# Second-level Strassen for one more product of the last down projection, early weight sums on VectorE, residual loads on GpSimd's queue

## The chip, the core and the metric

The kernel runs on one core of a Trainium2 chip. The core has TensorE for matmuls (the profile names it PE, and PEld for its weight loads), VectorE (DVE), ScalarE (ACT), GpSimd (POOL) and SyncE (SP), which here only issues DMAs. The metric is the device time of one execution in microseconds; less is better.

## The reference

For 2048 tokens of width 1024, with `_layernorm` over the width:

```python
xn = _layernorm(x)
s = linear_attention(xn, wqkv) @ wo          # 32 heads of 32
g = silu((silu(xn @ w_gate) * (xn @ w_up)) @ w_down)   # inner width 3584
return x + s * g
```

The first three of its lines are the reference's `_A_ref` and `_B_ref` in short; all inputs are bf16.

## The kernel before, in words

**Stages.** The first part (to about 245 us of the span) normalizes x, computes the attention branch and writes s to DRAM (`s_dram`). The feed-forward part then goes over the tokens in two passes of 1024. Each pass has a gate/up stage over 28 keys (14 column groups of 256, gate and up alternating; `emit_a`, `emit_c22`, `emit_b`, `emit_evac`) and a down stage. Every matrix product there is done by Strassen's scheme with 7 products of half size in place of 8: sums of the left operand are made by VectorE or GpSimd, sums of the weights are made once and kept in DRAM.

**The first down stage** (`emit_down`, 413.7 to 498.5 us) has an a-half with the four products that are kept or finished early and a b-half with the other three. Each half goes over two pairs of token tiles (hf). In a pair the second tile follows the first by 6 of 14 steps, so a pair has 20 steps (st); a step has one weight row group k of a tile. The b-half begins with pair hf = 1 at 462.2 us and goes on with hf = 0 at 480.3 us. Its banks come from two pools: four banks tagged "s" and two double banks tagged "d" (`dzw`). A tile's double bank is free when its evacuation (`evac_b`, line 1294 for hf = 1, which writes `dd`) has read it. Ahead of the b-half VectorE makes the left sums S1 to S4 of the next pass (`emit_Ssum`, lines 711 to 714).

**The last down stage** (`emit_down_m`, from 668.7 us) computes the seven products M1 to M7 one after the other, for four tiles t of 128 tokens each side. A product at one level is 4 tiles x 14 matmuls of 512 columns (line 1430). Products in `L2` (1, 2 and 4) use Strassen once more (`l2_M`, `l2_p`, line 1466): seven products of 14 matmuls of 256 columns each. `l2_M` is a generator: it stops after its first two products, so that another product can fill in. A second-level product needs four sums of its left operand (`l2_lhs`, lines 1163 to 1166, on GpSimd) and four sums of its weights. The order is M2 and M1 interleaved, M7, M6, M5, M4, M3. M3 is accumulated in M5's banks. Each finished tile goes through Silu on ScalarE and then `fin`.

**The residual** (`fin`, line 1200 to 1202, and `io_load`). For each of 32 tiles of 128 x 512, `fin` multiplies the gate by s (line 1200), adds x (line 1201), both on VectorE, and issues the store of the result; x and s were loaded by `io_load` into a buffer of two halves, and the result is written into the half that held x. Buffers come from a pool of five, "io"; a load goes into a buffer whose store has landed. Five loads are made ahead of the first down stage, and each `fin` issues the next. The last three tiles use the space of the sums S0 to S2 in place of a buffer of the pool. Stores of the first pass are issued by GpSimd (the last three of them are `deferred` into the first three keys of the last pass), stores of the last pass by SP. All loads are issued by SP.

**Early and late weight sums.** For M2 the second-level weight sums are made in the first down stage from weight tiles that are in SBUF anyway (`l2_early`, line 1132, on GpSimd, in steps 1, 3, ... of hf = 1, and stored with a lag of two weight tiles). For M1 and M4 the weights are loaded again in the last gate/up stage (`l2_load`, line 1111), summed by GpSimd (`l2_sums`, line 1144) and stored (line 1145). These loads take slots of the same pool of eight weight slots ("pk") as the weights of the keys.

**What sets the order.** TensorE, VectorE, ScalarE and GpSimd execute in the order of the program (`manual_schedule`), DMAs on GpSimd's queue among them. SP's order is chosen by the framework's planner in the feed-forward part. An instruction that waits holds up all that stand behind it on its engine.

Of the kernel before, what the change touches and what calls it, by code (L numbers as in the profile page):

```python
# [10 lines left out]
ALU = mybir.AluOpType  # L11
# [10 lines left out]
def kernel(  # L22
# [165 lines left out]
    passes = list(range(NPASS - 1, -1, -1))  # L188
    NWA = NFG // 2
    M_ORDER = (1, 2, 7, 6, 5, 4, 3)  # L190
    L2 = (1, 2, 4)
    L2_ORDER = (1, 2, 5, 6, 7, 4, 3)
    NQ = NFG // 2
    CH = CW // 2
# [757 lines left out]
    with ExitStack() as p3:  # L952
# [143 lines left out]
            eng.tensor_tensor(out=a21.bitcast(F16), in0=a12, in1=S2, op=ALU.subtract)  # L1096
            s_ring[(hf, m)] = (S1, S2, S3)

        l2_q = deque((M, j) for M in L2 if M != 2 for j in range(0, NQ, 2))
        l2_live = deque()  # L1100

        def l2_load():
            M, j0 = l2_q.popleft()
            kd, q = M_PACK[M]
            t = w_slot()
            v = t[:].rearrange("p h a b -> p (h a b)").rearrange("p (b j n) -> p b j n", b=8, n=CH)
            js = range(j0, min(j0 + 2, NQ))
            for j in js:
                for k, b0, b1 in ((0, 0, 7), (1, 1, 6)):
                    src = wd_drams[j][0 if kd == "a" else 1][:, k, q].rearrange("p (c n) -> p c n", n=CH)  # L1110
                    nc.sync.dma_start(out=v[:, b0:b1 + 1:b1 - b0, j - j0, :], in_=src)
            l2_live.append((M, js, v))

        def l2_early(M, j, store):

            t = w_tiles[(passes[0], "b", j)][:].rearrange("p h a b -> p (h a b)")
            q = M_PACK[M][1]
            w = t[:, 0:6 * CW].rearrange("p (k q c n) -> p q k c n", k=2, q=3, c=2)[:, q]
            T = t[:, 6 * CW:8 * CW].rearrange("p (b n) -> p b n", b=4)
            if store:  # L1120
                if M not in l2_drams:
                    l2_drams[M] = dram.tile([P, 7, NQ, CH], BF16, name="l2_%d" % M)
                d = l2_drams[M]
                nc.sync.dma_start(out=d[:, 0:2, j], in_=w[:, :, 0])
                nc.sync.dma_start(out=d[:, 6, j], in_=w[:, 1, 1])
                nc.sync.dma_start(out=d[:, 2:6, j], in_=T)
                return
            r = w.bitcast(F16) if M >= 4 else w
            t1, t2, t3, t4 = [T[:, i].bitcast(F16) for i in range(4)]
            for o_, a_, b_ in ((t1, r[:, 0, 1], r[:, 0, 0]), (t2, r[:, 1, 1], t1), (t3, r[:, 1, 1], r[:, 0, 1]),  # L1130
                               (t4, r[:, 1, 0], t2)):
                nc.gpsimd.tensor_tensor(out=o_, in0=a_, in1=b_, op=ALU.subtract)

        def l2_sums():
            M, js, v = l2_live.popleft()
# [8 lines left out]
                nc.gpsimd.tensor_tensor(out=b(o_), in0=b(a_), in1=b(b_), op=ALU.subtract)  # L1144
            nc.gpsimd.dma_start(out=l2_drams[M][:, :, js.start:js.stop, :], in_=v[:, 0:7, 0:n_, :])

        x_spare, r_spare = [], []

        def l2_bufs(M):
            v = [x[:].rearrange("p a b -> p (a b)").bitcast(F16) for x in x_spare]  # L1150
            if M == 1:
                v = [x[:].rearrange("p h a b -> p (h a b)").bitcast(F16) for x in r_spare]
            v = [x[:, 0:2 * NQ * 2 * P].rearrange("p (s j r n) -> p s j r n", s=2, j=NQ, r=2) for x in v]
            return [v[0][:, 0], v[0][:, 1], v[1][:, 0], v[1][:, 1]]

        def l2_quad(A, j):
            v = A[:, :, j].rearrange("p k (r t n) -> p k r t n", r=2, t=2)
            return v[:, 0, :, 0], v[:, 1, :, 0], v[:, 0, :, 1], v[:, 1, :, 1]

        def l2_lhs(M, A, j, eng):  # L1160
            a11, a12, a21, a22 = l2_quad(A, j)
# [22 lines left out]
        def io_load(after=None):  # L1184
            if not fq:
                return
            p, t, cc = key = fq.pop(0)
            r0 = p * TB2 + t * P
            pool, tg = (sp, "S%d" % len(fq)) if len(fq) < 3 else (iop, "io")
            io = pool.tile([P, 2, CW], BF16, name="io", tag=tg)  # L1190
            gate([nc.sync.dma_start(out=io[:, 0, :], in_=x2[r0:r0 + P, cc * CW:(cc + 1) * CW]),
                  nc.sync.dma_start(out=io[:, 1, :], in_=s_dram[r0:r0 + P, cc * CW:(cc + 1) * CW])],
                 after, sync=True)
            io_tiles[key] = io

# [10 lines left out]
        def emit_down(p, h, base, last, more_S, next_S):  # L1206
# [152 lines left out]
            for hf in (1, 0):  # L1359
                t0, t1 = 2 * hf, 2 * hf + 1  # L1360
                fresh = hf == 0
                endz = last and fresh
                for st in range(NFG if endz else NS):
                    if st == 4:
                        while pend:
                            pend.pop(0)()
                    if hf == 1 and not last and st % 2 == 1 and 2 in L2:
                        if st // 2 < NQ:
                            l2_early(2, st // 2, False)
                        if 0 <= st // 2 - 2 < NQ:  # L1370
                            l2_early(2, st // 2 - 2, True)
                    if st < NFG:
                        step_b(t0, st, fresh)
                        if st == NFG - 1:
                            fins = evac_b(t0, fresh)
                    if st >= LEAD and not endz:
                        step_b(t1, st - LEAD, fresh)
                        if fresh and (st - LEAD) % 2 == 1:
                            load_w_to(base + 2 * NWA + (st - LEAD) // 2 + 2)
                if endz:  # L1380
                    for f in fins:
                        f()
                    finish(t1)
                    break
                fins2 = evac_b(t1, fresh)
                for f in fins:
                    f()
                if fresh:
                    deferred.extend(fins2)
                else:  # L1390
                    for f in fins2:
                        f()

        def emit_down_m(p, h, base):
# [8 lines left out]
            def load(M, q=None):  # L1403

                n_ = max(i for i, key in enumerate(seq) if key[2][0] == M and q in (None, key[2][1])) + 1
                load_w_to(base + n_ + (NPK - 2 if M == 1 and q != 3 else NPK))

            def S3(k):
                return s3_[k // NWA][:, k % NWA]
# [59 lines left out]
            def l2_M(M, A, K, done, fill, in_place, dst=None):  # L1469
# [24 lines left out]
                for r in range(2):  # L1494
                    c0, c1 = c[r]
                    if K is None:
                        nc.scalar.copy(out=c1[:, hi], in_=zy[r][:, lo])
                        nc.scalar.copy(out=c0[:, hi], in_=zy[r][:, hi])
                        nc.scalar.copy(out=c0[:, lo], in_=xw[r][:, lo])
                    else:  # L1500
                        tt(c1[:, hi], zy[r][:, lo], K[2 * r + 1][:, hi])
                        tt(K[2 * r][:, hi] if in_place else c0[:, hi], zy[r][:, hi], K[2 * r][:, hi])
# [1 line left out]
                            tt(c0[:, lo], xw[r][:, lo], K[2 * r][:, lo])  # L1504
                    tt(c1[:, hi], xw[r][:, hi], c1[:, hi])
                fill()
                for r in range(2):
                    l2_p(M, 4, r, A, bk)
                load(M, 2)
                for r in range(2):  # L1510
# [2 lines left out]
                        nc.scalar.copy(out=c1[:, lo], in_=zy[r][:, lo])  # L1513
                    else:
                        tt(c1[:, lo], zy[r][:, lo], K[2 * r + 1][:, lo])
                        done(2 * r + 1, c1)
                    l2_p(M, 3, r, A, bk)
                    if in_place:
# [18 lines left out]
            load_w_to(base + NPK - 2)  # L1537
            KA = kept("kA")
            fins = deque()
            M7, M6, M5 = [], [], []  # L1540
            KB = []

            def fill7():
# [17 lines left out]
                flush(1)  # L1561
            load(7)
            sums(S4, A12, S2, ALU.subtract)
            for j in range(NQ):
                l2_lhs(4, quads(h, 1, 1), j, nc.gpsimd)
            M6 = banks()
            for t in range(TPB):
                prod_t(6, t, M6[t], True)
                tt(KB[t], M6[t], KB[t])
                tt(KA[t], M6[t], KA[t])  # L1570
            load(6)
            M5 = banks()
            for t in range(TPB):
                prod_t(5, t, M5[t], True)
                c = k2([P, CW], FP32, "c22")[:]
                tt(c, M5[t], KB[t])
                fins.append((t + TPB, 1, silu(c, "g22")))
                if len(fins) > 1:
                    flush(1)
            tt(KA[-1], M5[-1], KA[-1])  # L1580
            load(5)

            def out3(t):
                prod_t(3, t, M5[t], False)
                c = k2([P, CW], FP32, "c12")[:]
                tt(c, M5[t], KA[t])
                fins.append((t, 1, silu(c, "g12")))

            def done4(t, c):
                fins.append((t + TPB, 0, silu(c, "g21")))  # L1590

            def fill3():
                flush()
                out3(0)
            go(l2_M(4, quads(h, 1, 1), KB, done4, fill3, True))
            hs_ = [slice(0, 3 * CW // 4), slice(3 * CW // 4, CW)]
            out3(1)
            flush(len(fins) - 1)
# [15 lines left out]
        for pi, p in enumerate(passes):  # L1614
# [69 lines left out]

            na0 = 6 if first else 8
            l2_j = 0
            load_w_to(base + na0)
            if first:
                wd_pipe2(-1)
# [3 lines left out]
            for i in range(n):  # L1693
# [38 lines left out]
                if not first:  # L1732
                    if l2_live:
                        l2_sums()
                    if i in (17, 18):
                        r_spare.append(w_slot())
                    if i % 2 == 1 and l2_q:
                        l2_load()
                    if i >= 18 and 4 * l2_j + 4 <= i:
                        l2_lhs(1, quads(h, 0, 0), l2_j, nc.gpsimd)  # L1740
                        l2_lhs(2, quads(h, 1, 0), l2_j, nc.gpsimd)
                        l2_j += 1
                if deferred:
                    deferred.pop(0)()
            base += n
            if last_pass:
                l2_lhs(2, quads(h, 1, 0), NQ - 1, nc.gpsimd)
# [36 lines left out]
```

## Time and profile before

| | us |
|---|---|
| runs: median (lowest to highest of 3) | 758.43 (756.7 to 759.07) |
| the profiled execution | 756.18 |
| its span in the trace | 754.4 |
| first down stage, a-half / b-half hf = 1 / hf = 0 | 413.7 to 462.2 / to 480.3 / to 498.5 |
| last gate/up stage | 498.5 to 668.7 |
| last down stage, end of the last matmul | 668.7, 749.8 |

All times in the text are microseconds from the start of this span. A line of the profile names an engine, a source line of the kernel, an operation and its tiles (output <- inputs), and how many there were. In a waits view the numbers are the total, the number of waits and the longest. In a timeline they are start and duration, in brackets the engine's idle time before and what ended it. In a DMA view the last number is the median time from issue to landing. SPq and POOLq are DMA issues of these engines.

Other rows that matter here. The granted clock of TensorE is 1.00 in each stretch from 412 to 743.8. VectorE is busy 9.62 of the 18.3 us of hf = 1 of the b-half and 9.80 of the 18.2 us of hf = 0. The DMA engines are busy 0.38 of the a-half, 0.93 of hf = 1, 0.73 of hf = 0 and 0.92 of 498.5 to 523.

### The profile page before, as it was taken

The page shows a single profiled execution, that of the slowest core. Times are in us where ns is not written, and L with a number is a line of the kernel's source. Part 1 is how long each engine was busy: PE and PEld are TensorE (multiplying, and loading weights), DVE is VectorE, ACT ScalarE, POOL GpSimd, SP SyncE. Part 2 cuts the span into 40 slices and gives each one's busy share as a digit, 9 for nine tenths or more (in the row PEclk, how much of TensorE's full clock was granted, in tenths as well). Part 3 has the DMA queues.
Part 4 walks back from the last instruction along what each step waited for, and adds up shares of the span by engine and source line. Part 5 has one row for each costly group of instructions (what it writes and reads, how often), then busy time and mean ns, then how long its engine had stood idle before and what let it go on. Part 6 is the DMA issues. An engine that isn't in the chain of part 4 may idle for free.

```text
span 754.4 us, 11075 instructions
## 1 busy us (share of the span) xinstructions
PE 745.8 (99%) x3857; PEld 360.8 (48%) x3857; DVE 581.4 (77%) x1040; ACT 381.1 (51%) x545; POOL 399.8 (53%) x500
## 2 busy tenths in 40 slices
PE   8999999999999999999999999999999999999997
PEld 3544444454454444444444444444444444467464
DVE  6687787887697788888889785468776877687966
ACT  5677776889956575656658311132323222232023
POOL 2444799998540266868585021811542569434900
PEclk9999999999999999999999999999999999999999
DMA  9967799879779668878799228789786768479652
GB/s 318 304 146 139 228 332 298 303 158 271 206 190 296 231 214 301 295 279 316 273 323 409 111 65 306 222 295 339 258 306 222 281 206 344 147 258 318 209 161 77
DMA packets 129160, 187.77 MB, mean 249 GB/s; under 512 B 36208, under 2 KB 104176, under 8 KB 119376
## 3 DMA queue, kind: packets, MB, share of 16 engines
q1 hardware_dynamic: 121760, 156.00, 63.9%
q0 software_dynamic: 5904, 28.58, 9.9%
q10 hardware_dynamic: 1440, 2.49, 1.1%
q8 instruction: 30, 0.49, 0.3%
q14 instruction: 26, 0.21, 0.1%
HBM read 119.47 MB, written 60.23 MB: 238 GB/s over the span
## 4 chain that ended last, share of the span: by engine, by line
PE 84%; DMA 7%; POOL 3%; DVE 2%; issue 2%; ACT 1%; SPq 1%; POOLq 0%; DVEq 0%; ACTq 0%
PE zw L966 19%; PE kv_ps L554 15%; PE xb L966 10%; PE q_ps L183 6%; PE dzw L1228 6%; PE dm L1430 6%; PE yb L966 5%; PE dm L1466 4%; PE dx L1228 3%; DMA l<-w_sb 3%; PE fx L816 3%; DMA w_sb<-wd 3%; PE s_ps L774 3%; POOL w_sb L1144 2%; PE dy L1228 2%
## 5 line engine op out<-in xcount | busy, mean ns | idle before, releaser
L966 PEld LDWEIGHTS <-w_sb 128*128 128x128 f16 (+1 forms) x1568 | 152.1, 98 | 183.8 <-DMA w_sb<-pk_u 1.3
L966 PE MATMUL xb<-xnT,w_sb 128*128 128x512 bf16 x448 | 115.0, 379 | 0.0
L554 PE MATMUL kv_ps<-wkv_sb,xnT 128*128 128x512 bf16 x512 | 113.7, 379 | 0.6 <-ACT xnT L543 0.4
L966 PE MATMUL zw<-xnT,w_sb 128*128 128x512 bf16 x448 | 105.8, 379 | 0.0
L966 PE MATMUL zw<-S,w_sb 128*128 128x512 f16 x448 | 105.8, 379 | 0.0
L321 POOL TENSOR_TENSOR w_sb<-w_sb 128x512 f16<-128x512 bf16 x42 | 50.2, 1195 | 95.7 <-DVE w_sb L309 51.3
L286 ACT ACTIVATE w_sb<-w_sb 128x2048 bf16<-128x2048 bf16 x42 | 79.9, 1902 | 3.9 <-DMA w_sb<-in_B_w_up_dram 3.9
L554 PEld LDWEIGHTS <-xnT 128*128 128x128 bf16 x512 | 48.3, 97 | 56.0 <-ACT xnT L543 0.8
L1144 POOL TENSOR_TENSOR w_sb<-w_sb 128x512 f16<-128x512 bf16 (+3 forms) x32 | 35.4, 1126 | 52.4 <-DMA w_sb<-wd 51.9
L1042 ACT ACTIVATE sg<-cg 128x1024 bf16<-128x1024 f32 x28 | 29.6, 1057 | 57.4 <-DVE cg L1035 57.4
L183 PE MATMUL q_ps<-xnT,wq_sb 128*128 128x512 bf16 x256 | 58.4, 379 | 0.0
L966 PE MATMUL yb<-S,w_sb 128*128 128x512 f16 x224 | 57.4, 379 | 0.8 <-DMA w_sb<-pk_u 0.8
L1035 DVE SCALAR_TENSOR_TENSOR cg<-zw,rc_all,s 128x1024 f32<-128x1024 f32 x28 | 35.9, 1284 | 25.3 <-PE zw L966 13.2
L994 DVE SCALAR_TENSOR_TENSOR s<-yb,rc_all,s 128x512 f32<-128x512 f32 x42 | 31.5, 749 | 27.3 <-ACT s L993 27.3
L322 POOL TENSOR_TENSOR w_sb<-w_sb 128x512 f16<-128x512 bf16 x42 | 50.5, 1202 | 3.3
L324 POOL TENSOR_TENSOR w_sb<-w_sb 128x512 f16<-128x512 bf16 x42 | 50.3, 1197 | 0.0
L323 POOL TENSOR_TENSOR w_sb<-w_sb 128x512 f16<-128x512 bf16 x42 | 50.2, 1196 | 0.0
L1202 POOL DMA_DIRECT2D out_dram<-io x16 | 8.9, 555 | 69.2 <-DVE io L1201 69.0
L993 ACT ACTIVATE s<-xb,rcl 128x512 f32<-128x512 f32 x14 | 9.6, 687 | 66.3 <-PE xb L966 66.3
L1228 PE MATMUL dx<-w_sb,hT 128*128 128x512 bf16 x112 | 42.4, 379 | 0.0
L993 ACT ACTIVATE s<-xb,rc_all 128x512 f32<-128x512 f32 x42 | 28.4, 676 | 22.0 <-issue 12.7
L309 DVE TENSOR_SCALAR w_sb<-w_sb,cs_all 128x2048 bf16<-128x2048 bf16 x35 | 36.7, 1048 | 2.8
(213 smaller groups left out, 1351.1 us busy)
## 6 DMA issues: line engine op xcount, KB each, us to landing
w_sb<-pk_g SPq DMA_DIRECT2D x27, 1024.0 KB, 6.6
pk_g<-w_sb SPq DMA_DIRECT2D x14, 1024.0 KB, 5.0
w_sb<-pk_u SPq DMA_DIRECT2D x14, 1024.0 KB, 8.3
pk_u<-w_sb POOLq DMA_DIRECT2D x13, 1024.0 KB, 5.8
w_sb<-l SPq DMA_DIRECT2D x9, 896.0 KB, 4.6
w_sb<-in_B_w_gate_dram SPq DMA_DIRECT2D x14, 512.0 KB, 6.4
w_sb<-in_B_w_down_dram SPq DMA_DIRECT2D x28, 256.0 KB, 4.8
w_sb<-in_B_w_up_dram SPq DMA_DIRECT2D x14, 512.0 KB, 5.4
```

The lines of the kernel that those rows point to most:

```text
L183: nc.tensor.matmul(q_ps[:], lhsT=wq_sb[:, dc, g * P:(g + 1) * P], rhs=xn_ap(dc, btok), start=(dc == 0), stop=(dc == DC - 1))
L286: nc.scalar.activation(out=junk, in_=raw_view(key, t), func=ACT.Square, accum_out=asum[:])
L321: nc.gpsimd.tensor_tensor(out=T1, in0=b12, in1=b11, op=ALU.subtract)
L322: nc.gpsimd.tensor_tensor(out=T2, in0=b22, in1=T1, op=ALU.subtract)
L323: nc.gpsimd.tensor_tensor(out=T3, in0=b22, in1=b12, op=ALU.subtract)
L324: nc.gpsimd.tensor_tensor(out=T4, in0=b21, in1=T2, op=ALU.subtract)
L554: mm = nc.tensor.matmul(kv_ps[:], lhsT=xn_ap(dc, tok), rhs=wkv_sb[:, dc, c * CW:(c + 1) * CW], start=(dc == 0), stop=(dc == DC - 1))
L966: mm = nc.tensor.matmul(out, lhsT=lhs(k), rhs=rhs(k), start=(first and k == 0), stop=(k == HK - 1), skip_group_check=True)
L993: nc.scalar.activation(out=s1[:], in_=x_[:], func=ACT.Copy, scale=rc)
L1144: nc.gpsimd.tensor_tensor(out=b(o_), in0=b(a_), in1=b(b_), op=ALU.subtract)
L1228: nc.tensor.matmul(out, lhsT=lhs, rhs=rhs, start=first, stop=lastk, skip_group_check=True)
L1430: nc.tensor.matmul(out, lhsT=lhs_of(M)(k)[:, t * P:(t + 1) * P], rhs=w_of(M, k)[:, cols], start=first and k == 0, stop=k == NFG - 1, skip_ ...
```

## The change

- M5 becomes a second-level product too. Its left sums and those of M4 are made on VectorE by eight operations over all seven groups each (`l2_lhs_all`), in place of 28 GpSimd operations for M4. M5's and M4's generators are interleaved: M4's first two products run inside M5. M5's result goes to a buffer of its own (`T5`, in the space of S0 and S1) and is added to the kept sums KA and KB; M3 gets banks of its own. The four g22 tiles of M5 are finished together, inside M4.
- The second-level weight sums of M4 are made early too. They and those of M2 are made on VectorE, one group in each step of hf = 1 of the first down stage's b-half: M2's in steps 3 to 9, M4's in steps 10 to 16, with their stores 3 and 2 steps later. M4's sums overwrite the space of M2's.
- In the last gate/up stage M1's and M5's weights are loaded and summed, in two fixed slots of the weight pool, which afterwards hold the left sums of M1 and M5. M2's left sums are made along the stage, every fourth key. SP executes in the order of the program in this stage.
- Residual loads other than the first five are issued by GpSimd, and all use the five buffers.
- With M5, the weight tiles loaded ahead in the last down stage are limited to six until M5 is done (before: until M1 is done).

```diff
-    L2 = (1, 2, 4)
+    L2 = (1, 2, 4, 5)
+    L2_EARLY = (2, 4)
...
-            t = w_slot()
+            while len(r_spare) < 2:
+                r_spare.append(w_slot())
+            t = r_spare[len(l2_q) % 2]
...
-                nc.gpsimd.tensor_tensor(out=o_, in0=a_, in1=b_, op=ALU.subtract)
+                nc.vector.tensor_tensor(out=o_, in0=a_, in1=b_, op=ALU.subtract)
...
+        def l2_lhs_all(M, A, eng):
+            sb = l2_bufs(M)
+            for r in range(2):
+                v = A.rearrange("p k j (r t n) -> p k j r t n", r=2, t=2)[:, :, :, r]
+                a11, a12, a21, a22 = v[:, 0, :, 0], v[:, 1, :, 0], v[:, 0, :, 1], v[:, 1, :, 1]
+                s1, s2, s3, s4 = [x[:, :, r] for x in sb]
+                eng.tensor_tensor(out=s1, in0=a21, in1=a22, op=ALU.add)
+                eng.tensor_tensor(out=s2, in0=s1, in1=a11, op=ALU.subtract)
+                eng.tensor_tensor(out=s3, in0=a11, in1=a21, op=ALU.subtract)
+                eng.tensor_tensor(out=s4, in0=a12, in1=s2, op=ALU.subtract)
...
-            pool, tg = (sp, "S%d" % len(fq)) if len(fq) < 3 else (iop, "io")
+            pool, tg = iop, "io"
...
-            gate([nc.sync.dma_start(out=io[:, 0, :], in_=x2[r0:r0 + P, cc * CW:(cc + 1) * CW]),
-                  nc.sync.dma_start(out=io[:, 1, :], in_=s_dram[r0:r0 + P, cc * CW:(cc + 1) * CW])],
+            eng = nc.gpsimd if after is None else nc.sync
+            gate([eng.dma_start(out=io[:, 0, :], in_=x2[r0:r0 + P, cc * CW:(cc + 1) * CW]),
+                  eng.dma_start(out=io[:, 1, :], in_=s_dram[r0:r0 + P, cc * CW:(cc + 1) * CW])],
...
-                    if hf == 1 and not last and st % 2 == 1 and 2 in L2:
-                        if st // 2 < NQ:
-                            l2_early(2, st // 2, False)
-                        if 0 <= st // 2 - 2 < NQ:
-                            l2_early(2, st // 2 - 2, True)
+                    if not last:
+                        for M, q0, dq, lag in zip(L2_EARLY, (3, 10), (1, 1), (3, 2)):
+                            for d, store in ((0, False), (lag, True)):
+                                j, rem = divmod(st + (1 - hf) * NS - q0 - d, dq)
+                                if rem == 0 and 0 <= j < NQ:
+                                    l2_early(M, j, store)
...
-                load_w_to(base + n_ + (NPK - 2 if M == 1 and q != 3 else NPK))
+                load_w_to(base + n_ + (NPK - 2 if M in (1, 2, 7, 6, 5) and (M, q) != (5, 3) else NPK))
...
-                        nc.scalar.copy(out=c0[:, hi], in_=zy[r][:, hi])
-                        nc.scalar.copy(out=c0[:, lo], in_=xw[r][:, lo])
...
                 fill()
+                if K is None:
+                    for r in range(2):
+                        nc.scalar.copy(out=c[r][0][:, hi], in_=zy[r][:, hi])
+                        nc.scalar.copy(out=c[r][0][:, lo], in_=xw[r][:, lo])
...
-            for j in range(NQ):
-                l2_lhs(4, quads(h, 1, 1), j, nc.gpsimd)
+            l2_lhs_all(5, quads(h, 0, 1).bitcast(F16), nc.vector)
...
-            M5 = banks()
-            for t in range(TPB):
-                prod_t(5, t, M5[t], True)
...
+            l2_lhs_all(4, quads(h, 1, 1), nc.vector)
+            T5 = [sp.tile([P, 2, CW], FP32, name="kT", tag="S%d" % r) for r in range(2)]
...
+            def done5(t, T):
+                tt(KA[t], T, KA[t])
+                tt(T, T, KB[t])
...
             def fill3():
+                for t in range(TPB):
+                    fins.append((t + TPB, 1, silu(T5[t], "g22")))
                 flush()
+                M3.extend(banks())
                 out3(0)
-            go(l2_M(4, quads(h, 1, 1), KB, done4, fill3, True))
+            m4_ = l2_M(4, quads(h, 1, 1), KB, done4, fill3, True)
+            go(l2_M(5, quads(h, 0, 1).bitcast(F16), None, done5, lambda: next(m4_), False, T5))
+            go(m4_)
...
+            sp_man = ExitStack()
+            if last_pass:
+                sp_man.enter_context(tc.manual_schedule(engines={mybir.EngineType.SP}))
...
-                    if i in (17, 18):
-                        r_spare.append(w_slot())
-                    if i % 2 == 1 and l2_q:
+                    if i >= 3 and i % 2 == 1 and l2_q:
                         l2_load()
-                    if i >= 18 and 4 * l2_j + 4 <= i:
+                    if i >= 19 and 4 * l2_j + 4 <= i:
                         l2_lhs(1, quads(h, 0, 0), l2_j, nc.gpsimd)
-                        l2_lhs(2, quads(h, 1, 0), l2_j, nc.gpsimd)
                         l2_j += 1
+                    if i % 4 == 0 and i >= 4:
+                        l2_lhs(2, quads(h, 1, 0), i // 4 - 1, nc.gpsimd)
```

## The prediction

> **What bounds the kernel now.** I read the busy shares first, then the waits, then the chain in order of time.
>
> ```profile
> PE 745.8 (99%) x3857; PEld 360.8 (48%) x3857; DVE 581.4 (77%) x1040; ACT 381.1 (51%) x545; POOL 399.8 (53%) x500
> ```
>
> TensorE is busy 99% of the span, so time goes away only with matmuls or with the little idle time they have, and anything that makes TensorE wait is paid in full. The waits view lists what TensorE waits for in the part that the change touches:
>
> ```profile
> PE yb L966 <- DMA w_sb<-pk_u: 0.8, 1, 0.8
> ...
> PE dm L1466 <- ACT dm L1478: 0.3, 1, 0.3
> ```
>
> The first is at 623 us, a weight load held up by the second-level weight sums; the second is the start of M4. The chain of the last down stage gives the two paces:
>
> ```profile
> 668.88 18.34 PE dm L1466 x168
> ...
> 693.30 33.25 PE dm L1430 x154
> ```
>
> A 256-column matmul takes 18.34/168 = 0.1092 us, a 512-column one 33.25/154 = 0.2159 us. After the last matmul (749.8) a chain of VectorE and DMA runs to the end at 754.4.
>
> **1. M5 at the second level.** It has 4 x 14 = 56 matmuls at 0.2159 = 12.09 us; it becomes 7 products x 14 = 98 at 0.1092 = 10.70 us: **-1.4**. M4's first products now run inside M5, and the copies of M5 that stood ahead of M4's copy on ScalarE are moved behind it, so the 0.3 us wait goes: **-0.3**.
> What it needs: 16 sums on VectorE (128x896 f16) for M5 and M4. M4's 28 sums on GpSimd go, and GpSimd is then idle beside VectorE. In the VectorE timeline, sums of 128x1024 follow each other at 0.60 us when GpSimd rests (683.02 to 684.22) and at 1.08 us when it computes (694.57 to 701.02); 896 elements are by proportion 0.53 us. So S2 saves some 3 us and S4 and the four residual additions some 5 us; M5's 8 sums cost 4.2. M5's sums end near 712.8, M6 ends at 714.3: no wait. If the 1.08 pace stayed, they would end near 724, and M5 would wait some 4.5 us; I take none, since no GpSimd sum is left there.
>
> **2. Slots of the last gate/up pass.** Second-level loads keep two fixed slots; a weight load no longer takes a slot that they free. The number of loads and of GpSimd sums stays (M5 for M4, 8 loads of up to four DMAs). The 0.8 us wait goes: **-0.8**. SP is in program order there, and a load that waits for a slot holds up weight loads behind it; these have four keys (24 us) of lead, and the longest wait of that kind is 10.1 us, so nothing.
>
> **3. Early sums for M2 and M4, moved to VectorE.** 28 GpSimd sums (19.0 us) become 56 on VectorE in the b-half of the first down stage. The nearest row is a group of the same shape of dependence with 512 columns:
>
> ```profile
> 412.54 0.41 DVE L1093 TENSOR_TENSOR S<-hT 128x512 f16<-128x512 bf16 x1
> 412.99 0.42 DVE L1094 TENSOR_TENSOR S<-S,hT 128x512 f16<-128x512 f16 x1
> 413.33 0.42 DVE L1095 TENSOR_TENSOR S<-hT 128x512 f16<-128x512 bf16 x1
> 413.78 0.42 DVE L1096 TENSOR_TENSOR hT<-hT,S 128x512 f16<-128x512 bf16 x1
> ```
>
> Four take 1.59 us. Two dependent ones start 0.45 us apart, two independent ones 0.34, so a dependence adds 0.11. The last additions of the kernel (128 columns, dependent) start 0.25 apart at 751.4; between 0.25 and 0.45, 256 columns give 0.32 dependent and 0.21 independent. With one dependence a group takes **0.94 us**. In VectorE's order they stand behind the S sums of the next pass:
>
> ```profile
> 468.10 1.23 DVE L714 TENSOR_TENSOR xnT<-xnT,S 128x2048 f16<-128x2048 bf16 x1
> ...
> 476.05 1.22 DVE L1294 TENSOR_TENSOR dd<-dzw,s 128x1024 f32<-128x1024 f32 x1 [5.14 <-PE dzw L1228]
> 480.58 1.23 DVE L1294 TENSOR_TENSOR dd<-dzw,s 128x1024 f32<-128x1024 f32 x1 [3.31 <-PE dzw L1228]
> ```
>
> From 469.3: two residual tiles (1.6), eleven groups (10.3), then dd (1.15), which ends at 482.4, not 477.3. The next half's first zw bank is the one that dd frees, and TensorE wants it at 480.3: a wait of 2.1. Added to it: M4's group overwrites what M2's store still reads, and the DMA share between 462 and 480 is 0.93 already, while M4's stores add 21 DMAs (3.1 MB) to SP; stores issued at 465 to 471 there landed after 6 to 12 us. Bounds 0 (groups at 0.75 us or less fit) and 5; I take **+3.0**.
>
> **4. Residual loads on GpSimd's queue.** This is the large one. In the first pass the stores are on GpSimd's queue as well, and its order is the program's. There are five buffers, so load k+5 waits for store k to land, and store k+1 now stands behind that load. Today the stores follow each other at 0.55 to 0.8 us and SP does the waiting:
>
> ```profile
> SPq L1191 <- DMA out_dram<-io: 20.5, 9, 4.9
> ```
>
> After: one link = landing of a store + two issues (0.55 each). Landings of GpSimd's stores, in windows at 485, 494 and 501 us:
>
> ```profile
> out_dram<-io POOLq DMA_DIRECT2D x4, 128.0 KB, 2.7
> ...
> out_dram<-io POOLq DMA_DIRECT2D x1, 128.0 KB, 4.7
> ...
> out_dram<-io POOLq DMA_DIRECT2D x3, 128.0 KB, 7.8
> ```
>
> 2.7 with SP quiet, 4.7 beside one weight load, 7.8 beside seven. Weight loads will run from 490 on, some 2.6 us apart as slots come free, so I take 2.7 for store 5 and 4.7 for the next three, and 3.9 for a load (SP's at 488; GpSimd's loads are not in the trace). Store 5 at 488.2 (3 us late by part 3), load 10 issued by 492.1, load 11 by 497.9, load 12 by 503.7, load 13 by 509.5; it lands at 512.9. Tile 13's two VectorE operations stand before the evacuation of the first gate key, whose s3 then ends at 515.3. TensorE (next pass from 501.5) has 36 matmuls, 7.8 us, before it needs that: it waits from 509.3 to 515.3, **+6.0**. With 2.7 for all, nothing waits; with 6 for the later ones, 9. Behind it, the three deferred tiles follow at one link each, about a key's 6 us: nothing more.
> In the last pass stores go by SP and loads by GpSimd. Today the last three residual tiles have buffers of their own and are there by 667. Now each waits for an earlier store. Following VectorE: four additions of g22 end at 737.5 together with those of M4; SP's stores land in 1.7; the load of g12(0) is issued by 741.3 and lands near 743.3, wanted at 742.5; g12(1..3) land near 748.9, 750.0, 751.1 (2.5 for a load, SP's 2.2 to 2.6), the last wanted at 748.5. The last addition ends at 752.3, not 751.9, although TensorE ends 1.7 earlier: **+2.1**. Bounds 0 (loads in 1 us less) and 4 (each 2 us more).
> The Trainium skill's "DMA: Bandwidth & Descriptors", section "Anatomy of one DMA — SWDGE (gpsimd) path", gives 2.0 us plus bytes over 436e3 for a DMA of this queue: an estimate of 2.3 us for 128 KB. The quiet rows (2.0 at 443, 2.7 at 485) agree, the rows beside weight loads do not; by the page the 6.0 would vanish and the sum be +2.6. Its section "Issuing engines are not separate DMA queues" speaks against a gain by this edit: other queues save only issue time.
>
> **Sum.** -1.4 -0.3 -0.8 +3.0 +6.0 +2.1 = **+8.6 us**. The profiled execution took 756.18 (span 754.4 and 1.8 around it): 764.8. The median of the runs is 2.25 above that execution: **767.0**.
>
> **Rivals.**
> - **Everything hidden** (0.27): stores land in 2.7 us or less even beside weight loads, and the groups take 0.75 us. It decides at 2.7 because three links of 3.8 bring load 13 to 506.9, and TensorE's 509.3 is then met. For it: these loads go to another queue than SP's, where residual loads took 12 us behind weights, and SP frees earlier, so weights spread. Against it: the 4.7 and 7.8 rows. Price -2.5 to -0.4: 755.9 to 758.0, most of it no change, the edge faster.
> - **Only the sums on VectorE** (0.15): links short, part 3 as worked out: 8.6 - 6.0 = +2.6, 761.0; with 0 to 5 for part 3, 758 to 763.
> - **Worse** (0.08): links at 7.8, sums at 5, the tail at 4, M5's sums late: over 772.
> - **The forecast** (0.50): 762 to 772.
>
> TensorE has only 2.5 us to give, so faster is narrow. A difference of 0.3% (2.3 us) is about what can be told from none. Faster by more: 0.13, about half of the first rival. Same: 0.22, its rest and a part of the second. Slower: 0.65. The range 756 to 772 leaves out the last tenth of the first rival and the worse case.
>
> **What would show it.** Right: TensorE waiting for VectorE's dd at the middle of the b-half (2 to 5 us), VectorE idle before L1200 on DMA io by over 10 us in the first 20 us of the last pass, GpSimd's load lines waiting for out_dram's landing, TensorE idle before zw L966 there; M5 as 98 matmuls of 256 columns in 10.7 us; no wait for pk_u near 623; the last additions waiting for io. Wrong: landings under 3 us for GpSimd's stores while weights load; another order of stores and loads on GpSimd; groups at 0.75 us.

## The result, and the profile after

The changed kernel takes **775.88 us** (775.54 to 777.46, 4 runs), the kernel before beside it 757.57 (4 runs): ratio 1.0251 [1.0214, 1.0288], so 18.3 us slower. The profiled execution took 775.77 us, span 774.0, which is 19.6 above the span before. By stage, in microseconds of the two traces:

| | before | after | difference |
|---|---|---|---|
| start of the first down stage | 413.72 | 414.29 | +0.6 |
| first down stage | 84.79 | 86.52 | +1.7 |
| last gate/up stage | 170.21 | 183.92 | +13.7 |
| last down stage to the last matmul | 81.08 | 79.25 | -1.8 |
| last matmul to the end | 4.60 | 10.01 | +5.4 |

The page's line of TensorE, which was at 99% before:

```profile
PE 743.2 (96%) x3835; PEld 366.0 (47%) x3899; DVE 592.4 (77%) x1119; ACT 385.0 (50%) x557; POOL 385.6 (50%) x498
```

The waits of TensorE have two new rows on top, and the rows for pk_u and for M4's start are gone:

```profile
PE zw L967 <- DVE s L1009: 12.4, 1, 12.4
PE dzw L1242 <- DVE dd L1308: 1.8, 1, 1.8
```

**The large wait.** GpSimd's timeline of the changed kernel around it (start, duration, instruction, idle time before and what ended it):

```profile
487.86 0.55 POOL L1216 DMA_DIRECT2D out_dram<-io  x1 [7.18 <-DVE io L1215]
491.11 0.55 POOL L1205 DMA_DIRECT2D io<-in_A_x_dram  x1 [2.70 <-issue]
...
492.34 0.55 POOL L1216 DMA_DIRECT2D out_dram<-io  x1
500.08 0.55 POOL L1205 DMA_DIRECT2D io<-in_A_x_dram  x1 [7.19 <-DMA out_dram<-io]
...
501.16 0.55 POOL L1216 DMA_DIRECT2D out_dram<-io  x1
508.27 0.55 POOL L1205 DMA_DIRECT2D io<-in_A_x_dram  x1 [6.57 <-DMA out_dram<-io]
...
509.35 0.54 POOL L1216 DMA_DIRECT2D out_dram<-io  x1
514.96 0.55 POOL L1205 DMA_DIRECT2D io<-in_A_x_dram  x1 [5.07 <-DMA out_dram<-io]
```

Each load waits for the landing of the store issued just before it, and the next store stands behind that load. The first store landed 2.7 us after its issue, the next three after 7.45, 6.83 and 5.33. So the links are 9.0, 8.2 and 6.7 us long. VectorE is not what delays these landings: it rests from 490.7 to 498.6, while the store of 492.34 is under way. What stands beside them is in the DMA view of the changed kernel from 490 to 510 us (count, size, median time to landing): seven weight loads of 1 MB on SP's queue.

```profile
w_sb<-pk_u SPq DMA_DIRECT2D x4, 1024.0 KB, 9.1
w_sb<-pk_g SPq DMA_DIRECT2D x3, 1024.0 KB, 8.5
out_dram<-io POOLq DMA_DIRECT2D x3, 128.0 KB, 6.8
```

VectorE works through the residual tiles at the pace of the links and reaches the first gate key's evacuation (L995) only at 518.8, as its timeline shows:

```profile
517.95 0.43 DVE L1214 TENSOR_TENSOR g<-g,io 128x512 bf16<-128x512 bf16 x1 [2.72 <-DMA io<-s_dram]
...
518.75 0.74 DVE L995 SCALAR_TENSOR_TENSOR s<-yb,rc_all,s 128x512 f32<-128x512 f32 x1
```

TensorE stops at 508.75 and goes on at 521.19. The windows of the changed kernel over that stretch (busy time of each engine, then granted clock, DMA share, GB/s):

```profile
504.00:508.00 4.00, 4.00 (x20) 1.83 (x19) 0.85 (x2) 1.44 (x3) 0.00 (x0) 1.00 1.04 418
...
510.00:520.00 10.00, 0.00 (x0) 0.00 (x0) 2.76 (x6) 0.00 (x0) 3.15 (x6) 0.59 0.52 187
520.00:524.00 4.00, 2.81 (x7) 0.98 (x7) 3.26 (x5) 1.21 (x2) 1.71 (x4) 0.50 0.41 128
```

The DMA engines are full before 508. In the row of 510 to 520 TensorE does nothing, and its clock is halved from 511.81 to 525.46. Of that stretch 4.27 us lie after the restart, and at half speed they cost 2.1. So 12.4 + 2.1 - 0.8 (the wait for pk_u that is gone) = 13.7, the whole of the stage's difference.

**The early sums.** VectorE's timeline of the changed kernel:

```profile
472.32 9.39 DVE L1136 TENSOR_TENSOR w_sb<-w_sb 128x256 f16<-128x256 bf16 x40
481.63 1.22 DVE L1308 TENSOR_TENSOR dd<-dzw,s 128x1024 f32<-128x1024 f32 x1
```

Ten groups from 472.32 to 481.63 are 0.93 us each, and dd follows them at once: the 1.8 us row.

**M5 and the end.** The chain of the changed kernel in the last down stage:

```profile
730.46 11.48 PE dm L1481 x105
```

The 105 second-level matmuls from 730.46 belong to M5 and to the first two products of M4, which run inside it; they take 0.109 us each, with no wait ahead of them. The end, in VectorE's timeline of the same kernel:

```profile
760.25 0.43 DVE L1214 TENSOR_TENSOR g<-g,io 128x512 bf16<-128x512 bf16 x1 [1.55 <-DMA io<-s_dram]
...
764.23 0.68 DVE L1433 TENSOR_TENSOR c<-dm,kA 128x512 f32<-128x512 f32 x1
767.12 0.42 DVE L1214 TENSOR_TENSOR g<-g,io 128x512 bf16<-128x512 bf16 x1 [2.21 <-DMA io<-s_dram]
```

Twice here, and once more at 769.2, the additions wait for a residual load; the last addition ends at 771.1, 7.1 us after TensorE.

### The profile page after: what moved, and what is told of

Its sections match the earlier page's. It is cut to its first block, busy times and chain, and to the rows that moved or that the text cites. A ratio compares the mean times of both kernels' runs of the same rounds, so it can differ in the third digit from the quotient of the medians.

```text
span 774.0 us, 11176 instructions
## 1 busy us (share of the span) xinstructions
PE 743.2 (96%) x3835; PEld 366.0 (47%) x3899; DVE 592.4 (77%) x1119; ACT 385.0 (50%) x557; POOL 385.6 (50%) x498
## 5 line engine op out<-in xcount | busy, mean ns | idle before, releaser
L967 PE MATMUL zw<-xnT,w_sb 128*128 128x512 bf16 x448 | 107.5, 383 | 12.4 <-DVE s L1009 12.4
L967 PE MATMUL xb<-xnT,w_sb 128*128 128x512 bf16 x420 | 113.3, 379 | 1.5
L1205 POOL DMA_DIRECT2D io<-in_A_x_dram x27 | 14.8, 549 | 125.0 <-DMA out_dram<-io 61.9
L995 DVE SCALAR_TENSOR_TENSOR s<-yb,rc_all,s 128x512 f32<-128x512 f32 x42 | 31.4, 748 | 28.1 <-ACT s L994 28.1
```

The costliest lines, as they stand in the source:

```text
L967: mm = nc.tensor.matmul(out, lhsT=lhs(k), rhs=rhs(k), start=(first and k == 0), stop=(k == HK - 1), skip_group_check=True)
```

## The experiments

The theories for the large wait. **A**: it is the order of GpSimd's queue, in which stores and the loads that depend on them alternate. **B**: GpSimd's queue is slow for these transfers by itself. **C**: the early sums on VectorE push everything back. Ratios are to the kernel before, with a 95% interval.

**e1: all residual loads on SP again.** Changed kernel, with

```diff
-            eng = nc.gpsimd if after is None else nc.sync
+            eng = nc.sync
```

> The changed kernel with all residual loads issued by SP again; everything else of the change stays, the five buffers for all tiles too. Theory A (the chain on GpSimd's queue: store k+1 stands behind load k+5, which waits for store k to land) expects the 12.4 us wait of TensorE for the first gate key to be gone, with the half clock behind it (2.3 us), and loads at the end to come about 2 us earlier: 757 to 760. Theory B (GpSimd's DMAs are slow in themselves, 5 to 7 us each, in whatever order) expects the same here. Theory C (the early sums on VectorE push the residual tiles 4 us late, and the wait comes from that) expects most of the 12.4 us to stay: 766 or more.

Measured: **762.75 us**, 1.0074 [1.0046, 1.0101]. The 12.4 row is gone, the 1.8 row is still there, and there is a new wait for a weight load, at 504.7 us:

```profile
PE yb L967 <- DMA w_sb<-pk_u: 1.3, 1, 1.3
```

So C does not cause the large wait. The number is above the expectation mainly because the end stayed at 9.76 us (10.01 in the changed kernel). In e2 below, which keeps the loads on GpSimd's queue, it is 9.62, so that queue is not what makes the end long.

**e2: the first pass's stores on SP, the loads stay on GpSimd's queue.** Changed kernel, with

```diff
-            fin_e = (nc.vector, nc.vector, nc.sync if last else nc.gpsimd)
+            fin_e = (nc.vector, nc.vector, nc.sync)
```

> The changed kernel with the stores of the first pass issued by SP, and the residual loads left on GpSimd's queue: the loads there wait for landings as before, but no store stands behind a load. Theory A expects the wait at the first gate key gone or under 2 us, the end as slow as in the changed kernel: 760 to 763. Theory B expects tile 13 to come 5 to 7 us after its issue, in a row with the others, and a wait of 3 to 8 us left: 764 to 770. Theory C: 766 or more.

Measured: **760.46 us**, 1.0031 [1.0016, 1.0046]. GpSimd's timeline of e2:

```profile
492.49 0.55 POOL L1205 DMA_DIRECT2D io<-in_A_x_dram  x1 [16.51 <-DMA out_dram<-io]
...
493.56 0.55 POOL L1205 DMA_DIRECT2D io<-in_A_x_dram  x1
...
```

Five tiles' loads are issued one behind the other. All of these ten DMAs but the first still land 5.4 to 7.7 us after their issue, but side by side, and TensorE has no wait at the first gate key. That is A, and against B as the cause of the wait. Nor are slow landings special to GpSimd's queue: in the trace before, SP's residual load issued at 509.1 us landed after 12.4, and in e2 SP's stores issued at 503.7 to 505.3 after 13.3 to 14.2.

**e3: the queue edit alone, in the kernel before** (early sums on GpSimd, own buffers kept): in `io_load`, `nc.gpsimd` for all but the first five loads, as in the change.

> The kernel before with one edit of the change alone: residual loads other than the first five on GpSimd's queue (the last three keep their own buffers; the early sums for M2 stay on GpSimd). Theory A expects the chain here too, since stores and loads of the first pass share the queue: a wait of 8 to 13 us at the first gate key and the half clock behind it: 767 to 773. Theory B about the same or less. Theory C expects no wait: 757 to 760.

Measured: **785.88 us**, 1.0369 [1.0341, 1.0397], worse than the whole change and 13 us above the range of theory A. A's wait at the first gate key is there, and a second one ahead of it. The waits of TensorE in e3:

```profile
PE zw L966 <- DVE s L1008: 10.0, 1, 10.0
PE zw L966 <- DVE dd L1289: 8.3, 1, 8.3
```

GpSimd's own early sums run until 495.3 here, so the first store of the chain is issued 7.45 us later than in the changed kernel and the chain starts later. The second part of the change thus hides some of the third one's cost; the two were not independent, as the sum had them.

**e4: own buffers for the last tiles.** e1, with the last three tiles in S0 to S2 again and T5 elsewhere:

```diff
-            pool, tg = iop, "io"
+            pool, tg = (sp, "S%d" % len(fq)) if len(fq) < 3 else (iop, "io")
...
-            T5 = [sp.tile([P, 2, CW], FP32, name="kT", tag="S%d" % r) for r in range(2)]
+            T5 = xnp.tile([P, 4, CW], FP32, name="kT", tag="xn8")
...
```

> As the kernel with all residual loads on SP, and the last three tiles get buffers of their own again (space of S0 to S2); M5's result lies in the space that M7's left sums leave. Theory A for the end (the loads of the last tiles wait for stores because there are only five buffers) expects 2 to 3.5 us less than with the five buffers: 754.5 to 757. If the end is set by VectorE's backlog of additions and not by the loads, it is the same as with five buffers.

Measured: **760.45 us**, 1.0034 [1.002, 1.0048]. The end falls from 9.76 to 7.68 us; the run is 2.3 us below e1, as the theory has it, though its range, which counted on a faster e1, is missed. One wait is left in VectorE's timeline of e4, for the tile that is finished first and whose load was issued last:

```profile
748.67 0.43 DVE L1214 TENSOR_TENSOR g<-g,io 128x512 bf16<-128x512 bf16 x1 [2.60 <-DMA io<-s_dram]
```

**e5: three early sums moved into the a-half.** e2, with M2's first three groups in steps 14, 16 and 18 of the a-half's second pair, where VectorE rests.

```diff
+                    if hf == 1 and not last and st in (NFG, NFG + 2, NFG + 4):
+                        l2_early(2, (st - NFG) // 2, False)
...
-                                if rem == 0 and 0 <= j < NQ:
+                                if rem == 0 and 0 <= j < NQ and not (M == 2 and j < 3 and not store):
```

> e2 (the changed kernel with the first pass's stores on SyncE's queue, 760.5) with three of the early-sum groups of the last pass moved from the second half of the down stage into its first half. Theory 'VectorE's order': the 1.8 us for which TensorE waits at the down matmul for the addition dd is the seven groups of 0.93 us that stand ahead of it on VectorE, so with three of them gone from there the wait goes: 758.5 to 759.0. Rival 'dd waits for something else' (the down matmuls' own pace): 760.5, and the 1.8 us row stays.

Measured: **762.83 us**, 1.0074 [1.0053, 1.0096]: slower than e2, which no theory expected. The 1.8 row is gone, and a row of TensorE and VectorE's timeline in e5 say what took its place:

```profile
PE zw L967 <- DVE dd L1302: 2.8, 1, 2.8
```

```profile
500.73 0.43 DVE L1214 TENSOR_TENSOR g<-g,io 128x512 bf16<-128x512 bf16 x1 [13.17 <-DMA io<-s_dram]
...
501.54 1.22 DVE L1302 TENSOR_TENSOR dd<-dzw,kept 128x1024 f32<-128x1024 f32 x1
```

TensorE is 2.3 us earlier at the gate/up stage (498.15, e2 500.43; 0.3 of it was there at the start of the down stage), and now the next dd is late: it stands on VectorE behind the sixth residual tile, whose load landed at 500.7. The stop of 2.8 us also halves the clock from 503.10 to 506.51 (1.7 us more).

**e6: the end alone.** e2, with e4's buffers and one line that finishes the tile with the latest load last:

```diff
             go(m4_)
+            fins.rotate(-1)
```

> e2 with a buffer of its own for each of the last pass's last tiles (so that no load waits for a store) and with the final additions flushed in another order: the tiles whose residual came first are finished first, the one whose load is last comes last. Theory 'the end is five buffers and an order': the stretch from TensorE's last instruction to the end falls from 9.6 to about 5 to 7 us: 756.0 to 758.5. Rival 'the loads on GpSimd's queue are late by themselves': the end stays above 9 us, 760.

Measured: **755.77 us**, 0.9978 [0.9961, 0.9995]. The end is 4.93 us. By e4, 2.1 of the 4.7 gained are the buffers, so some 2.6 are the order; this is a difference, as no run changes the order alone.

**e7: e5 and e6 together.**

> e5's and e6's edits together: the stores of the first pass on SyncE's queue, three early sums earlier, own buffers and the other order at the end. If the costs add up: 754.5 to 756.5, some 1 to 3 us under the kernel before (757.6). If what is taken from one place is lost at the next: 758 to 760.

Measured: **757.88 us**, 1.0000 [0.9987, 1.0013]. It lies between the two ranges, next to the rival's, and the trace shows the rival's case: the same row as in e5 (2.3 us) with a half clock of 3.4 us.

**e8: the kernel before with loads on GpSimd's queue and the first pass's stores on SP** (e3 and e2's edit).

> The kernel before with two edits: residual loads on GpSimd's queue, as in e3 (785.9), and the first pass's stores on SyncE's. Theory 'store and load in one order': no load stands behind the landing of a store in its own queue, so the two rows of 10.0 and 8.3 us at the first gate keys go: 757 to 761. Rival 'GpSimd's queue is slow for these loads and its early sums keep them back': 770 or more, with the wait at the first gate key still there.

Measured: **761.97 us**, 1.0063 [1.0041, 1.0085], against e3's 785.88: taking store and load apart is worth 24 us. The number is 1 us above the theory's range: the row of 10.0 is gone, but of the row of 8.3 half is left. It is e5's row again:

```profile
PE zw L966 <- DVE dd L1289: 4.0, 1, 4.0
```

**e9: dd ahead of the sixth residual tile.** e7, with that tile's additions behind the next tiles' dd:

```diff
-                for f in fins:
+                for f in extra + fins:
...
+                    extra = fins2[2:]
+                    for f in fins2[:2]:
```

> e7 (757.9) with the two additions dd of the last down tiles put ahead of the sixth residual addition on VectorE, so that they do not stand behind that tile's load. Theory 'the wait moved to the next load': e7's row of 2.3 us at the first gate key, and the half clock behind it, go: 754.0 to 755.5. Rival 'the bank is late for another reason': 757.9, with the row still there. Against the kernel before (757.9 in the last job): 0.4 per cent faster by the theory.

Measured: **761.54 us**, 1.0043 [1.0025, 1.0062], a miss. TensorE now waits 5.8 us for the first gate key's evacuation:

```profile
PE zw L967 <- DVE s L1009: 5.8, 1, 5.8
```

VectorE's timeline of e9 shows why:

```profile
502.20 0.43 DVE L1214 TENSOR_TENSOR g<-g,io 128x512 bf16<-128x512 bf16 x1 [1.15 <-DMA io<-s_dram]
...
509.50 0.43 DVE L1214 TENSOR_TENSOR g<-g,io 128x512 bf16<-128x512 bf16 x1 [1.81 <-DMA io<-s_dram]
...
510.30 0.74 DVE L995 SCALAR_TENSOR_TENSOR s<-yb,rc_all,s 128x512 f32<-128x512 f32 x1
```

Four tiles, of which the first and the last are shown, stand ahead of the key; their loads land 2.3 to 2.6 us apart, the last 11.6 us after its issue, and the evacuation (L995) follows the last. The DMA share is 1.00 to 1.04 there.

**e12: no residual tile but one ahead of the first gate key.** e9, with the three tiles of the second-last down tile put among the deferred ones, one a key:

```diff
-                for f in extra + fins:
+                for f in extra if fresh else fins:
...
-                    deferred.extend(fins2)
+                    deferred.extend(fins + fins2)
```

> e9 (761.5) with the three residual tiles of the second-last down tile taken out of the stretch ahead of the first gate key too and put, one a key, with the three that already stood there. In e9 four tiles stood ahead of that key's evacuation on VectorE and their loads landed 7.6 to 11.6 us after issue, the last at 509.4. Theory 'VectorE waits in order behind loads that land late beside weight loads': with one tile left there, landing near 502, the wait of 5.8 us at the first gate key and the half clock behind it go: 753.5 to 755.5, faster than the kernel before (758.0). Rival 'the next one in line takes its place' (a weight load, or GpSimd's weight sums behind loads that wait for stores): 757 to 760 with a new row of waits.

Measured: **754.14 us**, 0.9958 [0.9945, 0.9971] (11 runs; before 757.36): 0.4% under the kernel before and faster than the changed one. From the first down stage on, this is the longest wait of TensorE that the view lists:

```profile
PE zw L967 <- DVE cg L1036: 0.2, 1, 0.2
```

The loads land as late as in e9, up to 11.3 us after their issue, and the clock is 1.00 up to 749.4. So a late landing alone does not stop TensorE; what counts is whether the key's evacuation stands behind it on VectorE. Against the trace before, the last gate/up stage is 0.6 us shorter, the last down stage 1.8.

**e10: M5 alone.** Loads on SP, M2's early sums on GpSimd, M4's weights loaded late like M1's. In this kernel the loads of twelve second-level sums (eight in the change) overwrite, as its code has it, the two buffers that hold M1's left sums, so M1 is computed from other data and waits for those loads.

> The second level for M5 alone: early weight sums for M2 on GpSimd and at their old steps, M4's sums where M1's and M5's are, residual loads on SyncE's queue, own buffers for the last tiles and the order of e6 at the end. Left out are the two other parts of the change. By the prediction's sum the part is worth 1.7 us, so with the end as short as before's 4.6 us: 755.5 to 757. If the added sums on GpSimd are late for the last down stage: a row of waits there and 760 or more.

Measured: 773.23 us, 1.0208 [1.0186, 1.0229], with this wait of TensorE on top:

```profile
PE dm L1481 <- POOL w_sb L1176: 12.5, 1, 12.5
```

The sums are late, as its second theory has it, but the shared buffers are part of that, so it prices nothing. M5's worth is read from the stage in the other traces: 79.25 to 79.26 us for that stage in e1, e2, e4, e6, e11 and e12, which have it, against 81.08 before and 81.07 to 81.08 in e3 and e8, which do not.

**e11: e6 with loads on SP and the first pass's stores on GpSimd's queue**, as in the kernel before.

> e6 (755.8) with the residual loads and the first pass's stores where they were before (loads on SyncE's queue, stores on GpSimd's). It prices the third part of the change by itself: if the loads on GpSimd's queue are worth the 1.3 us wait for pk_u that e1 showed, 757.0 to 757.8; if the queue of the loads makes no difference once no store stands behind them: 755.8.

Measured: **758.13 us**, 0.9998 [0.9985, 1.0011], 2.4 us above e6 and 0.3 above the range of the first theory. Two waits that e6 has not got fall at 510 and 503 us, where the residual loads stand on SP among the weight loads:

```profile
PE yb L967 <- DMA w_sb<-pk_g: 1.3, 1, 1.3
PE yb L967 <- DVE io L1215: 0.8, 1, 0.8
```

So the third part's idea, residual loads off SP's queue, is worth some 2 us (2.4 by the medians, 1.5 by the ratios) in this kernel, whose SP runs in program order there, once the stores are not in the same order; e11 moves loads and stores together, so the 2 us are those of the pair. The wait for pk_u at 623 us is not in e1 or e11 either.

## Why the prediction was wrong

The direction, the place and the mechanism of the large wait were right; 775.9 lies above the range, because two terms, the chain and the end, were less than half of what they are and the half clock had no term.

- **M5, -1.4 and -0.3: right.** Measured -1.8 in that stage. M5's sums on VectorE follow each other at 0.53 to 0.65 us, 4.5 in all where 4.2 was worked out, and ended in time.
- **pk_u, -0.8: right in number, the cause is open.** The wait at 623 us is gone here and in e1, e2, e11 and e12, whichever queue the residual loads use, which fits the prediction's slots. But e8, which keeps the old slots, has not got it either, so the slots are not shown to be the reason.
- **Early sums, +3.0: direction right, 1.8 measured.** A group takes 0.93 us (0.94 worked out) and the working gave 2.1; the part added on top, for buffers and stores, was not there.
- **Residual chain, +6.0: this step failed in size.** The words that failed are "I take 2.7 for store 5 and 4.7 for the next three". Store 5 took 2.7, the next three 7.45, 6.83 and 5.33: the first two of them are close to the third row, 7.8, which was seen at 501 us beside weight loads (six were under way in the trace, the prediction says seven). The reason given for the smaller row, 4.7 beside one weight load, was that weights would come 2.6 us apart. They were issued so (489.64, 491.94, 494.53, 497.12, then 1.3 apart), but each was under way for 7 to 13 us, so two, five and two of them were under way when the three stores were issued. The trace before had a sign of it: the single weight load beside its 4.7 us row took 6.9. Load 13 landed at 517.9 instead of 512.9 (5.0); TensorE waited for one more evacuation (0.8) and arrived 0.55 earlier: 6.0 + 6.4 = 12.4. The rival "worse" had the 7.8, at a chance of 0.08.
- **The half clock was in no term.** 2.1 us behind the wait of 12.4.
- **The end, +2.1: failed in size, one cause of two was missing.** It was worked out as an end 0.4 us later with TensorE 1.7 earlier; measured is +5.4 for the stretch, with TensorE 1.8 earlier. The five shared buffers, which the term is about, are worth 2.1 by e4. e6 puts some 2.6 on the order: the tile with the latest load is finished first. The prediction followed the loads' issue but not which tile VectorE takes first. With both mended, e6's end is within 0.3 us of the one before.
- The parts were summed as if independent. e3 shows that they are not: the queue edit alone costs 28 us, the whole change 18.

What stays open, besides pk_u: the 0.6 us by which the first down stage starts later in the changed kernel; it is smaller than the spread of that start over the runs' traces (412.98 to 414.47).

## What to carry to other kernels

Before a load and the store that frees its buffer are put on one in-order queue, write the queue's order out and multiply: each link costs a whole landing, and its length is read from a row with as many other loads under way, not from a quiet one. How many are under way follows from how long each takes to land, not only from how far apart they are issued. On the engine that computes, keep everything that waits for a transfer behind what TensorE waits for; e5, e7 and e9 show that to remove one wait there only brings the next transfer to the front, while e12, which moved the tiles themselves, ended it. Price a stop of TensorE with the half clock that follows; here each stop of 2.2 us or more had one.

## What the runs showed of the hardware

The clock also fell after stops shorter than 3.41 us. TensorE's stops and the half-clock stretches that came with them: 1.8 us (e2) none, 2.2 (e3) 3.41, 2.3 (e7) 3.41, 2.8 (e5) 3.41, 4.0 (e8) 6.83, 5.8 (e9) 6.83, 12.4 (changed kernel) 13.65. All stretches are multiples of 3.41 us; in e3's shortest stop, e5 and e7 the half clock began 0.3 us after TensorE had restarted, so the stop of 2.3 us cost 4.0 in all. The Trainium skill's "TensorE: Matmul & The Clock Gate", section "What's actually happening", gives a free-running window of 3413 ns, with which the multiples agree, and half speed after one idle window; here a stop of some two thirds of a window was enough, and the measurement decides. Stops between 1.8 and 2.2 us were not measured.

A load of 128 KB on GpSimd's queue took 2.3 to 2.5 us with no weight load under way (520 to 524 us in e9) and 6.7 to 11.6 us beside weight loads (e9, 494 to 509). The DMA share does not tell the two apart well: it was 0.90 in the first stretch and 1.00 to 1.04 from 500 to 512. From the DMA view of e9 from 520 to 527 us (the loads of x; count, size, median time to landing):

```profile
io<-in_A_x_dram POOLq DMA_DIRECT2D x4, 128.0 KB, 2.5
```

The 2.3 us that the prediction works out from the Trainium skill's "DMA: Bandwidth & Descriptors", section "Anatomy of one DMA — SWDGE (gpsimd) path", is the first case alone.
